# A transformer block in one kernel: where the up-projection's operands are read, split and kept

## The chip, the cores and the metric

The kernel runs on one core of one Trainium2 chip. The metric is device microseconds of one execution. Before the change three executions took 1883.05, 1883.9 and 1880.56 us, with a median of 1883.05 us. Times inside an execution are counted from the start of its span.

## The reference

The reference is one transformer block for 2048 tokens of width 1024, in fp32: linear attention with a learned feature map (32 heads of 32), then a dense layer with ReLU of width 3584. Both halves normalise first and add to their input.

```python
x = A_x
h = x + _A_ref(_layernorm(x), A_wqkv, A_w_phi, A_wo)
h2 = h + _B_ref(_layernorm(h), B_w1, B_w2)

# _A_ref: q, k, v = split(x @ wqkv); per head
phi_q = concat(softmax(q @ w_phi), softmax(-(q @ w_phi)))      # the same for k
o = phi_q @ (phi_k.T @ v) / (phi_q @ sum(phi_k) + 1e-6)        # then o @ wo
# _B_ref
relu(x @ w1) @ w2
```

## The kernel before

**Products in three parts.** Every fp32 operand is held as two fp32r parts: a high part, which ScalarE (ACT) writes as a rounded copy, and a low part, which VectorE (DVE) or GpSimd (POOL) writes as operand minus high part. A product is three matmuls (`mm3`): line 182 is high by high, 183 high by low, 184 low by high. Weights go through `Units`: SP loads a unit of 256 KB into one of six raw buffers, ACT writes its high part (line 125) and DVE or POOL its low part (line 129), into one of ten buffers. The load of a further unit waits until a raw buffer has been split.

**Stages.** Keys, values and queries come first, to about 520 us, then attention, then the output projection `wo` to 806 us. The up-projection runs from 806 to 1345 us and the down-projection to the end.

**The dense layer.** Both its products use a scheme of Strassen's kind: seven block products in place of eight. The normalised h is therefore kept as seven operands, the blocks 1, 5, 6, 2, 7, 3, 4 in the order of their first use (`UP`). Each block is 128 x 2 x 4 x 512 elements in SBUF (`hT[m]`: high and low part, four slices of 128 rows, 512 tokens). The tokens are worked in two halves. "First half" below is tokens 0 to 1023 (b = 0).

**How the first half's operands come about.** `ln_pair(i, stage)` takes two tiles of 128 tokens, for i = 0 to 3: it loads h, takes statistics, normalises, transposes on TensorE and forms the sums. `ln_store(i, j)` writes each of the seven results to DRAM (`hs[0, m]`, shape 128 x 4 x 4 x 128), for tile pair i. `h_load(0, m, g)` reads the two tile pairs 2g and 2g+1 of block m back into the low half of `hT[m]`; `h_high` (line 825, ACT) copies it to the high half, and `h_low` (line 829, DVE) subtracts that in place. TensorE reads all 512 tokens of both parts in every product, so both g have to be done before a block's second matmul.

The first half writes `hs[0, m][:, i]`: 2 KB of one partition in one piece. It reads with two transfers of 256 KB per `h_load`, and each of these writes pieces of 512 B into SBUF. The second half (`far_store`, line 805, and line 817) writes four pieces of 512 B per partition and reads with one transfer of 512 KB, in pieces of 1 KB.

**The order.** No scheduler reorders anything. `when(step, f, ...)` puts a call at a step, and a step is three matmuls. Each engine and the SP queue take their instructions in the order in which the calls are made, and wait in that order. After each step `W.advance` may issue a split and the next unit's load. `up0` is the up-projection's first step. The steps that the change touches are written as offsets from it:

```python
step = up0 + (8 * j + (-62, -32)[g] if j < 4 else 6 * (j - 4) + 10 + 2 * g)
high = up0 + (8 * j + (-48, -19)[g] if j < 4 else 6 * (j - 4) + 20 + 2 * g)
```

`j` counts the blocks in the order `UP`, so j = 4, 5, 6 are blocks 7, 3, 4. Each block is used for eight steps (two pairs of weight units p), so block j is needed first at step 8j. The low part is written 2 steps after the high one, or 5 for the last three blocks. The loads of weights that fall between, written as offsets of the same kind, stand at steps -31, -27, -23 and so on to -3, then 4, 8, 12, 16, 20, 24, 28. In the steps -39 to 1 the last items of `wo` also put in their additions (`wo_add`, line 691), their statistics (`far_stats`, lines 749 and 752), stores of h (line 698) and loads of x (line 658).

**Memory.** Pools are opened and closed in stages. A later pool lies on the bytes of earlier ones, and its tiles wait for the last use of the tiles beneath. The pool `hp` holds x and h of the output projection (`xh`, four buffers), one buffer of attention, the sums `s12` and `s4l`, and the statistics `hst` of the second half's tiles (eight of 48 B). Tiles take their place in the pool in the order in which they are first asked for, so `hst` lies last. On the same bytes the pool `mlp` later puts blocks 7, 3 and 4 and, behind them, `c11` and the other results of the up-projection. Before the change, block 4 lies on `xh`, the buffer of attention, `s12` and a part of `s4l`, and the first `c11` on the rest of `s4l` and on `hst`.

Of the kernel before, what the change touches and what calls it, by code (L numbers as in the profile page):

```python
# [9 lines left out]
F32 = mybir.dt.float32  # L10
# [5 lines left out]
P = 128  # L16
# [124 lines left out]
def kernel(  # L141
# [12 lines left out]
    v, act, pool, pe, sp = nc.vector, nc.scalar, nc.gpsimd, nc.tensor, nc.sync  # L154
# [18 lines left out]
    def f32(ap):  # L173
        return ap.bitcast(F32)
# [27 lines left out]
    hs = {(b, m): dram.tile([P, 4, 4, P], F32, name=f"hs{b}_{m}") for b in range(2) for m in UP}  # L202
# [535 lines left out]
    def ln_store(i, j):  # L738

        x1, x2 = (xnt["h", 4 * r + i] for r in range(2))  # L740
        s12, s4 = sums[0, i]
        m, t = ((1, x1[:, 0:512]), (5, s12[:, 0, :]), (6, s12[:, 1, :]), (2, x1[:, 512:]), (7, x2[:, 0:512]),
                (3, s4), (4, x2[:, 512:]))[j]
        sp.dma_start(hs[0, m][:, i], t.rearrange("p (k n) -> p k n", k=4))

    def far_stats(t, hf):
        if hf == 0:
# [6 lines left out]
    hst = {}  # L754
# [52 lines left out]
    sums, hT = {}, {}  # L807

    def h_load(b, m, g):

        cols = slice(2 * g * P, 2 * (g + 1) * P)
        if b == 0:
            lo = hT[m][:, 1, :, cols].rearrange("p k (i n) -> p k i n", i=2)
            for i in range(2):
                sp.dma_start(f32(lo[:, :, i, :]), hs[b, m][:, 2 * g + i])
            return
        sp.dma_start(f32(hT[m][:, 1, :, cols]), hs[b, m].rearrange("p k i n -> p k (i n)")[:, :, cols])

    def h_parts(m, g):
# [116 lines left out]
    def item(gen, *args, keys):  # L936
        items.append((gen, args + (keys,)))
        steps.extend((k,) for k in keys)
        return len(items) - 1
# [11 lines left out]
    for b, tiles in enumerate(groups):  # L951
        for hf in range(2):

            pairs = b == 0 and hf == 0
            for j in range(0, 4, 2 if pairs else 1):
# [3 lines left out]
                for half in range(2):  # L959
                    n = item(wo_pair, tiles[j:j + 2], hf, half, keys=[("wo", hf, 4 * half + k // 2) for k in range(8)])  # L960
# [26 lines left out]
    def when(step, f, *args):  # L987

        if step < 8 * first_up:
            do(step // 8, step % 8, f, *args)  # L990
        else:
            do(first_up + (step - 8 * first_up) // 4, step % 4, f, *args)
# [4 lines left out]
    for t in range(1, NT):  # L997
        n = t - 1 if t < HT else q_n[1, t - HT] + 1
# [62 lines left out]
    def to_wo():  # L1061
        nonlocal hp
        right.close()
        opool[1] = wos.enter_context(tc.tile_pool(name="oT1", bufs=1, side="right", reuse_waits="tile"))
        hp = wos.enter_context(tc.tile_pool(name="hp", bufs=2, side="right", reuse_waits="tile"))

    def to_far():
        far = wos.enter_context(tc.tile_pool(name="wofar", bufs=6, side="right", reuse_waits="tile"))
        W.far = Ring(far, 6, [P, 2, 512], F32R, "wf")
# [23 lines left out]
    do(q_n[0, 0], -1, to_half)  # L1093
    do(last_kv + 4, -1, to_attention)
    do(wo_first, -1, to_wo)
    do(wo_first + 2, -1, to_far)
    do(wo_n[12, 0], -1, to_ln2)
# [47 lines left out]
    up0 = 8 * first_up  # L1145
    when(up0 + 26, far_scale)
    for i in range(4):
        near, far = wo0 + 64 + 40 * i, up0 + 60 + 68 * i
        ln2 = NEAR.get(i, (0, 9, 12, 17, 24, 25, 26, 27, 29, 36))
        for stage in range(9):  # L1150
            when(near + ln2[stage], ln_pair, i, stage)
        for stage in range(7):
            when(far + FAR[stage], far_pair, i, stage)
        for j in range(7):
            when(near + ln2[9] + j // 2, ln_store, i, j)
            when(far + FAR[7] + j, far_store, i, j)
    assert wo_n[8, 0] + 10 < first_up

    def up_step(b, p, m):

        return up0 + 4 * (up_n[b, p, m] + 1 - first_up)

    for j, m in enumerate(UP):

        for g in range(2):
            step = up0 + (8 * j + (-62, -32)[g] if j < 4 else 6 * (j - 4) + 10 + 2 * g)
            high = up0 + (8 * j + (-48, -19)[g] if j < 4 else 6 * (j - 4) + 20 + 2 * g)
            when(step, h_load, 0, m, g)
            when(high, h_high, m, g)
            when(high + (2 if j < 4 else 5), h_low, m, g)  # L1170
            step = up_step(0, NP - 1, m) + 2 * j
            when(step + 3 * g, h_load, 1, m, g)
            when(step + 22 + 4 * g, h_high, m, g)
            when(step + 25 + 4 * g, h_low, m, g)
# [13 lines left out]
    for n, (w, p, j) in enumerate((w, p, j) for w in (1, 2) for p in range(NP) for j in range(2)):  # L1188
        step = sums_at[n]
# [7 lines left out]
    for b in range(2):  # L1197
        for m in DOWN:
            n = down_n[b, m, NP - 1] + 1
            name, more = {1: "x1", 5: "x4", 6: "x2", 4: "x3"}.get(m), \  # L1200
# [109 lines left out]
```

## Time and profile before

| | before |
|---|---|
| median of three executions | 1883.05 us |
| the profiled execution's own time | 1883.67 us |
| its span | 1881.9 us |
| TensorE busy | 1871.4 us (99%) |
| VectorE, GpSimd, ScalarE busy | 1070.6, 973.1, 739.0 us |
| DMA, mean over the span | 230 GB/s |

The profiled execution's own time is 1.8 us over its span. Rows in the prediction come from four kinds of views. A wait reads "engine line waited for: us in total, times, longest". A row of the order in time reads "start, length, engine, line, operation, out<-in, shapes, count", and in brackets how long the engine stood idle in front of it and what ended that. A row of a stretch reads "length, then for each engine busy us and instructions, then the granted TensorE clock (1.00 is full), the busy share of the DMA engines and GB/s". A group of one tile's instructions reads "line, engine, operation, out<-in, count: shortest/median/longest in ns, first and last start". "SPq" is the queue of the engine that issues the DMAs; its rows are the issue, not the transfer. A matmul's length overlaps with the next one's, so its cost is the distance between starts.

### The profile page before, as it was taken

How to read it: one execution, taken by the hardware profiler on the slowest of the kernel's cores; microseconds unless marked ns; L12 is line 12 of the kernel's file. 1: busy time of each engine (PE TensorE's matmuls, PEld its weight loads, DVE VectorE, ACT ScalarE, POOL GpSimd, SP SyncE). 2: the span in 40 equal slices, each digit the busy share in tenths (PEclk: the TensorE clock that was granted, in tenths of full speed). 3: DMA queues.
4: the chain of work that ended last, by engine and by line, in shares of the span. 5: the costliest groups of instructions: out<-in, count | busy, mean ns of one | idle time of the engine just before them, and what ended most of it. 6: DMA issues, size and time to landing. Idle time of an engine off the chain costs nothing.

```text
span 1881.9 us, 31799 instructions
## 1 busy us (share of the span) xinstructions
PE 1871.4 (99%) x11608; PEld 1535.3 (82%) x11608; DVE 1070.6 (57%) x1695; ACT 739.0 (39%) x1271; POOL 973.1 (52%) x959
## 2 busy tenths in 40 slices
PE   9999999999999999999999999999999999999999
PEld 7877788888787888878888888888888888888887
DVE  7788688677689777555554563444433333343333
ACT  5322245222233122255455554444444444444442
POOL 4887744888946988333233222222344444444443
PEclk9999999999999999999999999999999999999999
DMA  6888788656565666887888985666677677767775
GB/s 225 290 293 289 227 296 258 199 190 200 185 217 177 203 226 221 259 258 217 258 254 263 320 273 176 192 191 215 210 238 215 204 228 238 238 213 219 216 216 178
DMA packets 303277, 432.17 MB, mean 230 GB/s; under 512 B 24208, under 2 KB 165520, under 8 KB 303120
## 3 DMA queue, kind: packets, MB, share of 16 engines
q1 hardware_dynamic: 286224, 413.36, 70.0%
q10 hardware_dynamic: 16896, 16.78, 2.7%
q8 instruction: 91, 1.49, 0.3%
q14 instruction: 66, 0.54, 0.1%
HBM read 292.68 MB, written 137.36 MB: 229 GB/s over the span
## 4 chain that ended last, share of the span: by engine, by line
PE 95%; DMA 2%; POOL 1%; DVE 1%; issue 0%; ACT 0%; SPq 0%; DVEq 0%; ACTq 0%; POOLq 0%
PE mm L182 25%; PE mm L183 24%; PE mm L184 24%; PE ac L183 4%; PE ac L182 4%; PE ac L184 4%; PE tp L183 2%; PE tp L184 2%; PE tp L182 2%; PE tp L245 1%; PE ac L464 1%; PE tp L633 1%; DMA hT<-hs 1%; DMA hs<-xin 1%; PE ac L633 1%; POOL w L129 0%
## 5 line engine op out<-in xcount | busy, mean ns | idle before, releaser
L129 POOL TENSOR_TENSOR w<-raw,w 128x512 fp32r<-128x512 f32 x353 | 469.2, 1331 | 719.8 <-ACT w L125 674.8
L125 ACT ACTIVATE w<-raw 128x512 fp32r<-128x512 f32 x686 | 409.0, 626 | 508.0 <-PE mm L184 235.0
L129 DVE TENSOR_TENSOR w<-raw,w 128x512 fp32r<-128x512 f32 x333 | 271.4, 816 | 519.5 <-ACT w L125 514.1
L182 PE MATMUL mm<-w,xT 128*128 128x512 f32 x768 | 305.3, 398 | 0.0
L183 PE MATMUL mm<-w,xT 128*128 128x512 f32 x768 | 299.8, 390 | 0.6 <-POOL w L400 0.4
L184 PE MATMUL mm<-w,xT 128*128 128x512 f32 x768 | 299.3, 390 | 0.0
L183 PE MATMUL mm<-hT,w 128*128 128x512 f32 x672 | 262.1, 390 | 2.8 <-DVE hT L829 2.8
L182 PE MATMUL mm<-hT,w 128*128 128x512 f32 x672 | 262.2, 390 | 0.0
L184 PE MATMUL mm<-hT,w 128*128 128x512 f32 x672 | 262.0, 390 | 0.0
L362 POOL TENSOR_TENSOR b<-b 128x256 f32<-128x256 f32 x176 | 143.5, 816 | 55.1 <-DMA b<-in_w_dram 36.9
L182 PEld LDWEIGHTS mm<-w,xT 128*128 128x128 f32 x768 | 144.2, 188 | 33.9 <-issue 2.9
L184 PEld LDWEIGHTS mm<-w,xT 128*128 128x128 f32 x768 | 144.2, 188 | 30.7
L183 PEld LDWEIGHTS mm<-w,xT 128*128 128x128 f32 x768 | 144.3, 188 | 29.9 <-POOL w L129 1.0
L182 PE MATMUL mm<-w 128*128 128x512 f32 x392 | 152.5, 389 | 0.0
L183 PE MATMUL mm<-w 128*128 128x512 f32 x392 | 152.5, 389 | 0.0
L184 PE MATMUL mm<-w 128*128 128x512 f32 x392 | 152.5, 389 | 0.0
L183 PEld LDWEIGHTS mm<-hT,w 128*128 128x128 f32 x672 | 126.6, 188 | 29.6 <-DVE hT L829 3.3
L184 PEld LDWEIGHTS mm<-hT,w 128*128 128x128 f32 x672 | 126.6, 188 | 26.4
L182 PEld LDWEIGHTS mm<-hT,w 128*128 128x128 f32 x672 | 126.4, 188 | 26.3
L182 PEld LDWEIGHTS mm<-w 128*128 128x128 f32 x392 | 73.6, 188 | 15.3
L183 PEld LDWEIGHTS mm<-w 128*128 128x128 f32 x392 | 73.6, 188 | 15.3
L184 PEld LDWEIGHTS mm<-w 128*128 128x128 f32 x392 | 73.6, 188 | 15.2
(184 smaller groups left out, 3147.9 us busy)
## 6 DMA issues: line engine op xcount, KB each, us to landing
raw<-t SPq DMA_DIRECT2D x224, 256.0 KB, 3.9
raw<-ad SPq DMA_DIRECT2D x196, 256.0 KB, 3.0
raw<-in_w_dram SPq DMA_DIRECT2D x168, 256.0 KB, 3.1
ad<-c SPq DMA_DIRECT2D x112, 256.0 KB, 3.6
b<-in_w_dram SPq DMA_DIRECT2D x44, 512.0 KB, 6.0
t<-b SPq DMA_DIRECT2D x44, 512.0 KB, 4.8
ad<-s SPq DMA_DIRECT2D x84, 256.0 KB, 3.9
ed<-qe ACTq DMA_DIRECT2D x32, 512.0 KB, 4.4
```

Of the source, the lines that this page charges most:

```text
L125: nc.scalar.activation(w[:, 0, :], raw[1], AF.Copy)
L129: eng.tensor_tensor(out=w[:, 1, :], in0=raw[1], in1=w[:, 0, :].bitcast(F32), op=ALU.subtract)
L182: pe.matmul(ps, a_hi, b_hi, start=first, stop=False, skip_group_check=more)
L183: pe.matmul(ps, a_hi, b_lo, start=False, stop=False, skip_group_check=more)
L184: pe.matmul(ps, a_lo, b_hi, start=False, stop=last, skip_group_check=more)
L245: pe.transpose(pt[:, k, :], xn[:, (4 * j + k) * P:(4 * j + k + 1) * P], ident)
L362: pool.tensor_tensor(out=tsum[*u, *out], in0=tsum[*u, *a], in1=tsum[*u, *b], op=ALU.subtract)
L464: pe.matmul(kv_ps[s][g][32 * i:32 * (i + 1), 0:64], vt[:, 32 * h:32 * (h + 1)], phi[:, 64 * h:64 * (h + 1)], start=first, stop=last)
L633: pe.matmul(banks[g][32 * c:32 * (c + 1), j * P:(j + 1) * P], kvL[rows, 4 * q + 2 * sd + h // 4, 32 * (h % 4):32 * (h % 4 + 1)], phT_of[u ...
```

## The change

There are five edits. (1) The first half's stores write `hs[0, m][:, :, i]`, so the four slices of a tile pair lie apart. (2) The special form of `h_load` for b = 0 goes, and every read is one transfer of 512 KB. (3) The second reads (g = 1) of the first four blocks stand at -29 in place of -32, and their high parts at -15 in place of -19, so 14 steps behind the read. (4) The reads of the last three blocks stand 6 steps sooner and their high and low parts 2 steps sooner, so the high part is again 14 steps behind the read. (5) `to_wo` asks for one `hst` tile at once, so that the statistics take the first bytes of `hp`; block 4 then lies on the statistics, and the first `c11` exactly on `s4l`.

```diff
-        sp.dma_start(hs[0, m][:, i], t.rearrange("p (k n) -> p k n", k=4))
+        sp.dma_start(hs[0, m][:, :, i], t.rearrange("p (k n) -> p k n", k=4))
...
         cols = slice(2 * g * P, 2 * (g + 1) * P)
-        if b == 0:
-            lo = hT[m][:, 1, :, cols].rearrange("p k (i n) -> p k i n", i=2)
-            for i in range(2):
-                sp.dma_start(f32(lo[:, :, i, :]), hs[b, m][:, 2 * g + i])
-            return
         sp.dma_start(f32(hT[m][:, 1, :, cols]), hs[b, m].rearrange("p k i n -> p k (i n)")[:, :, cols])
...
         hp = wos.enter_context(tc.tile_pool(name="hp", bufs=2, side="right", reuse_waits="tile"))
+        hp.tile([P, 2, 6], F32, name="hst", bufs=8)
...
-            step = up0 + (8 * j + (-62, -32)[g] if j < 4 else 6 * (j - 4) + 10 + 2 * g)
-            high = up0 + (8 * j + (-48, -19)[g] if j < 4 else 6 * (j - 4) + 20 + 2 * g)
+            step = up0 + (8 * j + (-62, -29)[g] if j < 4 else 6 * (j - 4) + 4 + 2 * g)
+            high = up0 + (8 * j + (-48, -15)[g] if j < 4 else 6 * (j - 4) + 18 + 2 * g)
             when(step, h_load, 0, m, g)
             when(high, h_high, m, g)
             when(high + (2 if j < 4 else 5), h_low, m, g)
```

## The prediction

> **What bounds the kernel now.** I read the page's busy times first, then the waits of TensorE (engine, line, what it waited for: total us, times, longest), then stretches of the span (length, busy time and instructions of each engine, clock, DMA share, GB/s), then the order of single instructions in the stretch that stands out.
>
> ```profile
> PE 1871.4 (99%) x11608; PEld 1535.3 (82%) x11608; DVE 1070.6 (57%) x1695; ACT 739.0 (39%) x1271; POOL 973.1 (52%) x959
> PE mm L183 <- DVE hT L829: 2.8, 1, 2.8
> PE tp L1229 <- POOL ones L1225: 1.6, 1, 1.6
> PE tp L245 <- ACT xn L238: 1.3, 1, 1.3
> 799.00:846.00 47.00, 44.16 (x217) 35.89 (x216) 26.70 (x35) 25.33 (x38) 18.61 (x20) 0.96 0.87 262
> 846.00:893.00 47.00, 47.00 (x209) 38.93 (x208) 27.61 (x34) 23.67 (x43) 15.29 (x11) 1.00 0.76 214
> ```
>
> TensorE is busy 1871.4 of 1881.9 us; apart from the first microseconds its one long wait is for hT, the up-projection's operand, at the subtraction of line 829. The stretch that holds this wait is also the one with a clock under 1.00. So the change can gain there and nearly nowhere else; everything else it does can only add a wait of TensorE.
>
> ```profile
> 828.80 0.39 PE L182 MATMUL mm<-hT,w 128*128 128x512 f32 x1
> 832.03 0.50 PE L183 MATMUL mm<-hT,w 128*128 128x512 f32 x1 [2.84 <-DVE hT L829]
> 836.24 0.39 PE L182 MATMUL mm<-hT,w 128*128 128x512 f32 x1
> 836.48 0.39 PE L183 MATMUL mm<-hT,w 128*128 128x512 f32 x1
> 832.00:836.00 4.00, 3.97 (x10) 3.15 (x11) 4.00 (x5) 3.36 (x5) 1.13 (x1) 0.57 1.07 305
> ```
>
> **What the stall costs.** Matmuls start 0.23 us apart (836.24 to 836.48), so the one at 832.03 was due at 829.03: 3.00 us. Behind it the granted clock is 0.57 for 4.00 us, which loses 4.00 x 0.43 = 1.72 us. Together 4.7 us, if the subtraction is ready by 829.03 and no clock is lost.
>
> It is block 7 (step 32 after the up-projection's start at 806.21; a step is three matmuls, 0.68 us). Why it is late, on SP, ACT and DVE:
>
> ```profile
> 813.11 5.22 SPq L337 DMA_DIRECT2D raw<-t  x2
> 818.43 0.93 SPq L815 DMA_DIRECT2D hT<-hs  x2
> SPq L337 <- DVE w L129: 4.4, 1, 4.4
> 813.75 0.60 ACT L852 ACTIVATE c<-mm 128x512 f32<-128x512 f32 x1 [2.78 <-DVE mv L752]
> 824.93 1.06 ACT L825 ACTIVATE hT<-hT 128x1024 fp32r<-128x1024 f32 x1 [4.24 <-DMA hT<-hs]
> 827.40 1.06 ACT L825 ACTIVATE hT<-hT 128x1024 fp32r<-128x1024 f32 x1 [0.93 <-DMA hT<-hs]
> 828.37 0.61 ACT L125 ACTIVATE w<-raw 128x512 fp32r<-128x512 f32 x1
> 829.01 0.69 DVE L129 TENSOR_TENSOR w<-raw,w 128x512 fp32r<-128x512 f32 x1 [9.33 <-ACT w L125]
> 829.62 2.35 DVE L829 TENSOR_TENSOR hT<-hT 128x1024 fp32r<-128x1024 f32 x2
> ```
>
> SP issues one weight load at 813.11, then stands 4.4 us, because the next one needs a raw buffer that a DVE split frees; the reads of block 7 stand behind that load. They land about 6 us after issue, ACT copies the high parts at 824.93 and 827.40, and DVE subtracts until 831.97, behind a split that waits for ACT. In front of this, ACT's first take of c11 waited 2.78 us for line 752: the far tiles' statistics, whose bytes c11 reuses.
>
> **The change, part by part.** (1) Last three blocks. Loads go 6 steps sooner: block 7 from steps 10 and 12 to 4 and 6, block 3 to 10 and 12, block 4 to 16 and 18. In SP's written order the weight load of step 8, the one that waits 4.4 us, now comes behind block 7. So block 7 follows the issue at 813.11: about 813.5 and 814.0, not 818.43 and 819.96.
>
> ```profile
> L815 SPq DMA_DIRECT2D hT<-hs x28: 370/498/1534, 764.3 to 830.6; - x28
> L817 SPq DMA_DIRECT2D hT<-hs x14: 524/530/810, 1048.8 to 1091.5; - x14
> L825 ACT ACTIVATE hT<-hT x28: 1043/1051/1063, 773.6 to 1104.8; 128x1024 fp32r<-128x1024 f32 x28
> L829 DVE TENSOR_TENSOR hT<-hT x28: 1201/1218/2320, 775.0 to 1107.7; 128x1024 fp32r<-128x1024 f32 x28
> DMA to landing us min/median/max: 5.5/7.0/8.6
> ```
>
> The last line is of the 14 whole-size reads of the second half (line 817), the form that the first half now takes: 7.0 us median, 8.6 worst. From 814.0 that is 821.0 to 822.6. Then ACT: high, a split, high, a split (1.05 + 0.61 + 1.05 + 0.61 = 3.3, partly before the second landing, so some 2.3 behind it), and DVE 0.69 + 1.22: done at 825.2 to 826.8. Due is 829.03, so 2.2 to 3.8 us are left; with the longest subtraction of the row (2.32) still 1.1. The last two blocks follow by 8 steps (5.4 us) each and have the same lead. What is passed: the weight loads of steps 8 to 24 come behind up to three reads (0.53 us of issue each); their splits stand at steps 32 and later and their use at 60 and later, so 2 us there cost nothing. If that cover were gone, it would be those 2 us.
>
> (2) One read in place of two: 14 x (2 x 0.498 - 0.530) = 6.5 us of SP's time less, spread over 764 to 831. The stores must now scatter:
>
> ```profile
> L744 SPq DMA_DIRECT2D hs<-xin x16: 320/426/1196, 680.8 to 791.8; - x16
> L805 SPq DMA_DIRECT2D hs<-xin x16: 519/630/1027, 892.5 to 1032.9; - x16
> 790.00:800.00 10.00, 10.00 (x46) 8.29 (x45) 3.32 (x5) 2.39 (x4) 3.18 (x3) 1.00 1.02 343
> 824.00:830.00 6.00, 5.19 (x52) 3.77 (x50) 0.99 (x2) 3.88 (x7) 0.00 (x0) 1.00 1.11 302
> ```
>
> The second half's stores already have the new form (line 805): 0.2 us more of SP each, 28 x 0.2 = 5.7 us, in four bursts of seven. In the queue, mostly 2 KB pieces move at 343/1.02 = 336 GB/s, mostly 512 B pieces at 302/1.11 = 272. Seven stores of 0.26 MB take 5.5 us at the one and 6.7 at the other: up to 1.2 us per burst, less what reads in 1 KB pieces give back. None of the first three bursts has a reader soon; the fourth (785 to 792) counts in (3).
>
> (3) First four blocks, second halves: loads 3 steps later, high and low 4 later. On SP the read of block 1 passes a weight load and a load of x; on ACT its high part lets one split go first; on DVE its subtraction passes an addition with its statistics. Block 1 is needed at 806.43.
>
> ```profile
> 806.43 0.39 PE L183 MATMUL mm<-hT,w 128*128 128x512 f32 x1
> 796.20 0.69 DVE L691 TENSOR_TENSOR xh<-mm,xh 128x512 f32<-128x512 f32 x1 [8.41 <-DMA hd<-xh]
> 800.81 1.22 DVE L829 TENSOR_TENSOR hT<-hT 128x1024 fp32r<-128x1024 f32 x1 [1.15 <-ACT hT L825]
> 802.44 0.69 DVE L691 TENSOR_TENSOR xh<-mm,xh 128x512 f32<-128x512 f32 x1 [0.40 <-DMA hd<-xh]
> 803.16 0.70 DVE L749 BATCH_NORM_STATS2 hst<-xh 128x6 f32<-128x512 f32 x1
> 803.96 0.21 DVE L752 BATCH_NORM_AGGREGATE mv<-hst 128x2 f32<-128x12 f32 x1
> 804.09 0.64 DVE L129 TENSOR_TENSOR w<-raw,w 128x512 fp32r<-128x512 f32 x1
> ```
>
> Now the subtraction runs at 800.81, ahead of the addition at 802.44. Behind it, it starts when the split starts now, 804.09, and ends at 805.3: 1.1 us before 806.43. The high part fits: a read about 2 us later than now lands near 802 and is copied by 803. The addition starts when an earlier store of h lands; up to 1.2 us from (2) leaves 0 to 1.1 us. I cost it at nothing, with the bounds 0 and, if the store lands 2 us late, a gap of 0.9 plus 1.72 of clock, 2.6 us. Blocks 5, 6 and 2 follow by 8 steps each, with the same additions in front, and have more room. A gain is excluded: TensorE waits for nothing there now.
>
> (4) Statistics' place. No instruction more. c11 no longer lies on the statistics but on a sum stored about 791, so ACT's 2.78 us go. Block 4's tile now lies on the statistics, last read at 813.7; its load comes about 818. I take nothing beyond (1): the ACT wait is no wait of TensorE, and my 813.5 does not use it. The moved buffers of x and h serve a stage in which TensorE never waits.
>
> **Sum.** The profiled execution took 1883.67 us (span 1881.9): 1883.67 - 4.7 = 1879.0. The median of the three runs, 1883.05, is 0.6 lower: 1878.4.
>
> [...] The 2.84 us gap is followed by the clock of 0.57. [...] Here the row decides: every other 47 us stretch up to the kernel's end has 1.00, and gaps of 0.3 and 0.5 us (next fence) left it at 1.00.
>
> ```profile
> 470.00:517.00 47.00, 46.71 (x321) 37.13 (x320) 32.06 (x62) 12.56 (x23) 42.87 (x45) 1.00 0.58 183
> 564.00:611.00 47.00, 46.54 (x610) 37.49 (x623) 45.67 (x76) 15.10 (x27) 31.07 (x34) 1.00 0.54 182
> ```
>
> **Rivals.**
> A (my forecast): the stall goes, nothing takes its place. 1878.4. Chance 0.58.
> B: a smaller wait comes in its place, at 806 for block 1 or 812 for block 5, for the reason in (3). For: 0 to 1.1 us of room, DMA share about 1. Against: fewer issues, and ACT is freed earlier. 0.3 to 2.6 us: 1878.7 to 1881.0, with two such gaps 1882. Chance 0.21.
> C: the clock falls all the same. 1883.05 - 3.0 = 1880.05. Against: the fall stands directly behind the gap. Chance 0.04.
> D: the change does not do what it says; block 7 still lands late, because the queue is full, not SP held (DMA share near 1 around it). Then the 5 us of earlier issue shrink to under 2: a stall of 1 us or more with its clock, 1880.5 to 1883. Against: a wait of SP for a buffer, not for a landing, stands in front of the reads. Chance 0.06.
> E: slower. One mechanism: the addition ahead of block 1's subtraction waits for its store as the one at 796.20 did, 8.41 us in place of 0.40. The subtraction then ends at 813.3, a gap of 6.9 plus 1.72, less 4.7: +3.9, 1887.0. It decides from a gap of 3.0 on (no gain left). For: the moved read and the scattered stores sit in the same queue. Against: now it waits 0.40. Chance 0.11.
>
> **Numbers.** 0.2%, about what a measurement tells from no change, is 3.8 us. A is 0.25%; the three runs spread over 3.3 us, so I let one in six of A read as no change: faster 0.58 x 0.83 = 0.48, plus a third of B (0.07): 0.55. Same: 0.10 of A, 0.13 of B, C, D: 0.33. Slower: E and a trace of B, 0.12. Range: A's own is 1875.9 (1880.56 - 4.7) to 1880.5; with B, C and D it reaches 1884, and E stays out.
>
> **What would show it.** The wait of line 183 for line 829 at 829 gone, clock 1.00 in all stretches; block 7's reads issued right behind one weight load about 813 to 814; no ACT wait of a c11 take for line 752; block 1's last subtraction at 804 to 806.4. I am wrong if TensorE waits for line 829 near 806 or 812, or if a clock below 1.00 stays.

## The result, and the profile after

| | before | after |
|---|---|---|
| median | 1882.36 us (20 executions, 1880.56 to 1885.7) | 1879.31 us (20 executions, 1879.11 to 1879.53) |
| the profiled execution's own time | 1883.67 us | 1879.26 us |
| its span | 1881.9 us | 1877.5 us |

The ratio is 0.9983, with a 95% interval of 0.9976 to 0.999: the change makes the kernel 3.05 us faster (0.16%). Forecast were 1878.4 us and a gain of 0.25%. The time lies in the predicted range, 0.9 us above the forecast. By the bound of 0.2% that the prediction set, the gain counts as no change (which it gave a chance of 0.33, and faster 0.55), although the interval leaves 1 out.

Two differences have to be kept apart. The two profiled executions differ by 4.4 us, near the 4.7 us of the prediction's sum. The medians differ by 3.05. The experiments tell why.

The page and the waits of TensorE in the kernel after (engine, line, what it waited for: total us, times, longest), all that the trace has:

```profile
PE 1869.3 (100%) x11608; PEld 1533.9 (82%) x11608; DVE 1070.9 (57%) x1695; ACT 739.3 (39%) x1271; POOL 973.0 (52%) x959
PE tp L245 <- ACT xn L238: 1.6, 1, 1.6
PE tp L1225 <- POOL ones L1221: 1.6, 1, 1.6
PE tp L633 <- POOL ez L575: 0.5, 1, 0.5
PE mm L183 <- POOL w L400: 0.4, 1, 0.4
PE mm L183 <- POOL w L129: 0.3, 1, 0.3
```

The wait of 2.8 us for hT is gone, and no wait for hT has come in its place. Up to these places the code has five lines fewer, so lines 815 and 817 of before are 812 now, 825 is 820, 829 is 824, and 852 is 847.

The stretch that had clock 0.96 before, and the order in time on TensorE, SP, ACT and DVE (start, length, engine, line, operation, tiles, shapes, count, idle time in front):

```profile
799.00:846.00 47.00, 47.00 (x238) 38.72 (x237) 29.78 (x36) 27.22 (x41) 19.29 (x18) 1.00 0.88 288
```

```profile
806.56 0.39 PE L183 MATMUL mm<-hT,w 128*128 128x512 f32 x1
...
829.15 0.39 PE L183 MATMUL mm<-hT,w 128*128 128x512 f32 x1
```

```profile
812.07 0.32 SPq L337 DMA_DIRECT2D raw<-t  x1
812.48 1.20 SPq L812 DMA_DIRECT2D hT<-hs  x2
813.77 0.62 SPq L337 DMA_DIRECT2D raw<-t  x1
SPq L337 <- POOL w L129: 3.4, 1, 3.4
```

```profile
810.58 0.58 ACT L847 ACTIVATE c<-mm 128x512 f32<-128x512 f32 x1
...
818.58 1.06 ACT L820 ACTIVATE hT<-hT 128x1024 fp32r<-128x1024 f32 x1
```

```profile
803.88 1.20 DVE L824 TENSOR_TENSOR hT<-hT 128x1024 fp32r<-128x1024 f32 x1
...
824.13 1.22 DVE L824 TENSOR_TENSOR hT<-hT 128x1024 fp32r<-128x1024 f32 x1
```

TensorE's busy time fills the 47 us and the clock is 1.00. On SP both reads of block 7 are out by 813.7. The weight load behind them goes out at 813.77 without the 4.4 us in which the one before stood. SP is not free of such waits: the next weight load then stands 3.4 us for a split of POOL (the last row, a wait between 814 and 819), but block 7's reads are past it. ACT's first take of c11, at 810.58, has no wait in brackets; the high part of block 7's first half starts at 818.58, 6.3 us sooner than before. On DVE the subtraction of block 1 runs at 803.88. DVE finishes block 7 at 824.13 + 1.22 = 825.35, and TensorE uses it at 829.15: it has 3.8 us of room where it was 3.0 late.

### The profile page after: what moved, and what is told of

The parts are those of the page before. It is cut to its first block, busy times and chain, and to the rows that moved or that the text cites. A ratio compares the mean times of both kernels' runs of the same rounds, so it can differ in the third digit from the quotient of the medians.

```text
span 1877.5 us, 31764 instructions
## 1 busy us (share of the span) xinstructions
PE 1869.3 (100%) x11608; PEld 1533.9 (82%) x11608; DVE 1070.9 (57%) x1695; ACT 739.3 (39%) x1271; POOL 973.0 (52%) x959
## 4 chain that ended last, share of the span: by engine, by line
PE 98%; POOL 1%; DVE 0%; DMA 0%; ACT 0%; issue 0%; SPq 0%; POOLq 0%; ACTq 0%
PE mm L182 25%; PE mm L183 25%; PE mm L184 25%; PE ac L182 4%; PE ac L184 4%; PE ac L183 4%; PE tp L182 2%; PE tp L184 2%; PE tp L183 2%; PE tp L245 1%; PE ac L464 1%; PE tp L633 1%; PE ac L633 1%; POOL w L129 0%; PE tp L290 0%; PE mm L290 0%
```

## The experiments

The theory under test (the order theory): block 7's operand is late because its reads stand in SP's order behind a weight load that waits for a buffer. Rivals are that ACT's wait for the statistics passes the delay on, that the form or the number of the transfers makes it, and that the gain has another source than this stall. Unless said otherwise, each experiment is the kernel before with one edit.

### The last three blocks' steps alone

```diff
-            step = up0 + (8 * j + (-62, -32)[g] if j < 4 else 6 * (j - 4) + 10 + 2 * g)
-            high = up0 + (8 * j + (-48, -19)[g] if j < 4 else 6 * (j - 4) + 20 + 2 * g)
+            step = up0 + (8 * j + (-62, -32)[g] if j < 4 else 6 * (j - 4) + 4 + 2 * g)
+            high = up0 + (8 * j + (-48, -19)[g] if j < 4 else 6 * (j - 4) + 18 + 2 * g)
```

> Only the steps of the last three blocks are changed; stores, reads, the first four blocks and the statistics stay as before. My theory (block 7 is late because its reads are written behind the weight load that waits for a raw buffer): block 7's reads follow the weight load issued about 813, the wait of line 183 at 829 is gone, clock 1.00, and the time is that of the full change, 1879.3 us, 3 us under before. Rival A (the head of the delay is ACT's 2.78 us wait of the first c11 take for the statistics, and everything behind it is late in any order): ACT's wait is still there at about 811 to 814, block 2's high part comes behind it, and a wait of 0.5 to 2 us stays at 829: 1880.5 to 1882. Rival T (the pairs of 256 KB reads are what is slow): two reads of block 7 still land 2 us or more apart and the wait shrinks only by a half.

Measured: 1879.22 us (10 executions, 1878.92 to 1879.83) against 1881.7, ratio 0.9984 (0.9974 to 0.9993). It is as fast as the whole change. SP, ACT and DVE in order of time:

```profile
812.92 0.38 SPq L337 DMA_DIRECT2D raw<-t  x1
813.39 2.47 SPq L815 DMA_DIRECT2D hT<-hs  x4
817.77 0.33 SPq L337 DMA_DIRECT2D raw<-t  x1
```

```profile
813.55 0.60 ACT L852 ACTIVATE c<-mm 128x512 f32<-128x512 f32 x1 [2.67 <-DVE mv L752]
```

```profile
824.93 1.22 DVE L829 TENSOR_TENSOR hT<-hT 128x1024 fp32r<-128x1024 f32 x1
```

The four reads (two halves of block 7, two transfers each) are out ahead of the weight load, which still has to stand until 817.77. The low part ends at 826.15, 3.8 us ahead of its use at 829.91 in this trace. ACT's wait for the statistics is still there, 2.67 us, and the reads still have the old form. So neither of these has to go for the stall to end: the order alone is enough. The edit also moves the high and low parts, by two steps or 1.4 us; that is less than the 3.8 us of room, so the reads decide.

### All edits but that one

```diff
-        sp.dma_start(hs[0, m][:, i], t.rearrange("p (k n) -> p k n", k=4))
+        sp.dma_start(hs[0, m][:, :, i], t.rearrange("p (k n) -> p k n", k=4))
...
-        if b == 0:
-            lo = hT[m][:, 1, :, cols].rearrange("p k (i n) -> p k i n", i=2)
-            for i in range(2):
-                sp.dma_start(f32(lo[:, :, i, :]), hs[b, m][:, 2 * g + i])
-            return
...
+        hp.tile([P, 2, 6], F32, name="hst", bufs=8)
...
-            step = up0 + (8 * j + (-62, -32)[g] if j < 4 else 6 * (j - 4) + 10 + 2 * g)
-            high = up0 + (8 * j + (-48, -19)[g] if j < 4 else 6 * (j - 4) + 20 + 2 * g)
+            step = up0 + (8 * j + (-62, -29)[g] if j < 4 else 6 * (j - 4) + 10 + 2 * g)
+            high = up0 + (8 * j + (-48, -15)[g] if j < 4 else 6 * (j - 4) + 20 + 2 * g)
```

> Everything of the change but the steps of the last three blocks, which stay at 10 and 20. My theory: the reads stand behind the weight load of step 8 again; if that load waits about as long as before, the stall stays at 2 to 3 us and the time is that of before, 1882.4. Rival A (edit 5 frees ACT, which frees the raw buffer): the weight load goes out about 814 and block 7 is read about 814.5 and 815.5, so its low part is done before 829 with or without the earlier steps: 1879.3, as the full change. In the trace of the changed kernel that weight load goes out at 813.77, which speaks for A.

Measured: 1879.67 us (1879.14 to 1880.56), ratio 0.9988 (0.9979 to 0.9998), and no wait of TensorE for hT in the profile. The expectation that the stall stays fell. SP and DVE:

```profile
811.97 2.00 SPq L337 DMA_DIRECT2D raw<-t  x2
814.06 0.53 SPq L812 DMA_DIRECT2D hT<-hs  x1
...
818.18 0.32 SPq L337 DMA_DIRECT2D raw<-t  x1
818.55 0.53 SPq L812 DMA_DIRECT2D hT<-hs  x1
```

```profile
826.49 2.35 DVE L824 TENSOR_TENSOR hT<-hT 128x1024 fp32r<-128x1024 f32 x2
```

Here the weight load still stands ahead of block 7's reads, but it waits under 2 us, so the first half's read goes out at 814.06, 4.4 us sooner than before. The low part needs both halves, though, and the second half's read still stands behind a wait of SP (3.5 us, for a split of POOL): it goes out at 818.55, 1.4 us sooner than before, as one transfer that lands 5.7 us after issue. Before, the second of its two transfers went out at 820.4 and landed 6.9 us after issue. The low part ends at 828.84, 0.3 us ahead of its use. So the stall also ends without the earlier steps, by several smaller gains together. Rival A has the time right, but its second read was to go out at 815.5, and the statistics alone, further down, give nothing. Three single parts were then tried.

### Single reads with the stores that they need

```diff
-        sp.dma_start(hs[0, m][:, i], t.rearrange("p (k n) -> p k n", k=4))
+        sp.dma_start(hs[0, m][:, :, i], t.rearrange("p (k n) -> p k n", k=4))
...
-        if b == 0:
-            lo = hT[m][:, 1, :, cols].rearrange("p k (i n) -> p k i n", i=2)
-            for i in range(2):
-                sp.dma_start(f32(lo[:, :, i, :]), hs[b, m][:, 2 * g + i])
-            return
```

> Only the stores' form and the single 512 KB reads are changed; steps and statistics stay as before. Rival T (the transfers): block 7's second half lands about 1 us sooner behind its issue, and SP has 0.45 us less per read to issue; with fewer transfers in flight block 2 is also read sooner. The stall falls to 1 us or less: 1880 to 1880.7. My theory: the weight load of step 8 still holds SP to 817 or so, block 7 lands about 824 to 825.5, the low part ends about 830: a stall of 1 to 2 us, with or without the clock, 1880.5 to 1882.4. Slower than before by more than 1 us would mean that the scattered stores cost by themselves.

Measured: 1880.59 us (1880.13 to 1881.08), ratio 0.9992 (0.9983 to 1.0001). The stall is shorter, and no execution lost clock. SP and TensorE:

```profile
812.11 4.55 SPq L337 DMA_DIRECT2D raw<-t  x2
816.76 0.53 SPq L812 DMA_DIRECT2D hT<-hs  x1
```

```profile
830.02 0.50 PE L183 MATMUL mm<-hT,w 128*128 128x512 f32 x1 [0.76 <-DVE hT L824]
```

SP is still held for 4 us, but comes to it a microsecond sooner, and the read follows at 816.76 in place of 818.43. The gap is 0.76 us in place of 2.84, so by the size of the gap rival T came, although SP is held as the order theory had it. The form of stores and reads is thus a cause of a part of the stall, and the order is not the only one.

### The first four blocks' second halves alone

```diff
-            step = up0 + (8 * j + (-62, -32)[g] if j < 4 else 6 * (j - 4) + 10 + 2 * g)
-            high = up0 + (8 * j + (-48, -19)[g] if j < 4 else 6 * (j - 4) + 20 + 2 * g)
+            step = up0 + (8 * j + (-62, -29)[g] if j < 4 else 6 * (j - 4) + 10 + 2 * g)
+            high = up0 + (8 * j + (-48, -15)[g] if j < 4 else 6 * (j - 4) + 20 + 2 * g)
```

> Only the second reads of the first four blocks and their high and low parts are moved, in the old form of two reads. My prediction took this as worth nothing. Theory now: it frees ACT for one split before block 1's high part, so SP is not held 3 us at 800 and comes 1 us sooner to the reads behind; the stall at 829 shrinks by at most 1 us: 1880.5 to 1882. If it costs, a wait of line 183 near 806 shows up. The rival that this edit is the larger half of what the change gains without the last three blocks would show as 1879.5 to 1880.

Measured: 1880.19 us (1879.37 to 1882.08), ratio 0.9989 (0.9979 to 0.9999), no execution with lost clock. SP in order of time, and the wait of TensorE (total us, times, longest):

```profile
814.80 0.87 SPq L337 DMA_DIRECT2D raw<-t  x2
815.77 0.93 SPq L815 DMA_DIRECT2D hT<-hs  x2
```

```profile
PE mm L183 <- DVE hT L829: 0.6, 1, 0.6
```

The two weight loads go out one behind the other, and block 7's first read follows at 815.77, 2.7 us sooner than before. SP still stands in front of them, but 2.9 us in place of 4.4, and for a split of POOL. Why it no longer stands there for DVE is seen on DVE. The split whose buffer SP waits for, and the subtraction of block 2 next to it, in the kernel before:

```profile
816.16 1.23 DVE L829 TENSOR_TENSOR hT<-hT 128x1024 fp32r<-128x1024 f32 x1 [2.44 <-ACT hT L825]
817.30 0.69 DVE L129 TENSOR_TENSOR w<-raw,w 128x512 fp32r<-128x512 f32 x1
```

And in this experiment (the first row is the split, the second block 2's subtraction):

```profile
813.93 1.40 DVE L129 TENSOR_TENSOR w<-raw,w 128x512 fp32r<-128x512 f32 x1 [0.30 <-ACT w L125]
816.66 1.23 DVE L829 TENSOR_TENSOR hT<-hT 128x1024 fp32r<-128x1024 f32 x1 [1.33 <-ACT hT L825]
```

Before, the split stood behind a subtraction that waited 2.44 us for its high part. Four steps later, high part and subtraction come behind the split, which runs 3.4 us sooner and frees SP's buffer. The half that ends last gains less from this: its second transfer goes out at 819.9 in place of 820.4, behind another wait of SP for POOL (2.2 us), but lands 5.7 us after issue in place of 6.9; why it lands faster is not shown. So an edit to the first four blocks, whose operands are never late, is worth 1.8 us in the medians through block 7, between the 1 us that was expected at most and the rival's 1879.5 to 1880 us.

### The statistics' place alone

```diff
+        hp.tile([P, 2, 6], F32, name="hst", bufs=8)
```

> Only the statistics' place is changed (one line). Rival A: the c11 take runs about 811 instead of 813.75, the split behind it and so the weight load of step 8 come up to 2.8 us sooner, block 7's low part ends about 829.2 instead of 832.0: the stall shrinks to 0 to 0.5 us without loss of clock, 1879.3 to 1880. My theory in its strict form (order alone): block 2's high part still waits for its read at 815, so the split behind it and the load move by less than 1 us; a stall of 2 us or more stays, 1881 to 1882.4.

Measured: 1882.22 us (1880.43 to 1883.9), ratio 1.0002 (0.9992 to 1.0011). ACT, SP and TensorE:

```profile
810.97 0.58 ACT L852 ACTIVATE c<-mm 128x512 f32<-128x512 f32 x1
814.65 1.06 ACT L825 ACTIVATE hT<-hT 128x1024 fp32r<-128x1024 f32 x1 [3.10 <-DMA hT<-hs]
```

```profile
812.99 4.93 SPq L337 DMA_DIRECT2D raw<-t  x2
818.01 0.94 SPq L815 DMA_DIRECT2D hT<-hs  x2
```

```profile
831.14 0.50 PE L183 MATMUL mm<-hT,w 128*128 128x512 f32 x1 [1.96 <-DVE hT L829]
```

ACT's take of c11 no longer waits, but ACT then waits 3.10 us for a read that it had to wait for anyway. SP's order is as before, and the stall is there. The wait of 2.78 us stood in front of another wait; taking it away moved the read of block 7 by 0.4 us and the time by nothing that can be told from no change.

### The last three blocks' steps later

```diff
-            step = up0 + (8 * j + (-62, -32)[g] if j < 4 else 6 * (j - 4) + 10 + 2 * g)
-            high = up0 + (8 * j + (-48, -19)[g] if j < 4 else 6 * (j - 4) + 20 + 2 * g)
+            step = up0 + (8 * j + (-62, -32)[g] if j < 4 else 6 * (j - 4) + 14 + 2 * g)
+            high = up0 + (8 * j + (-48, -19)[g] if j < 4 else 6 * (j - 4) + 24 + 2 * g)
```

> The kernel before with reads, high and low parts of the last three blocks 4 steps (2.7 us) later. My theory of the clock (a longer gap makes the loss of clock more frequent): the gap grows to 3.5 to 5.5 us, nearly every run has the lowered clock (3.4 us at half, 1.7 us lost), and the time is 1.5 to 5 us over before: 1883.5 to 1887. Rival (the clock is lost by chance, whatever the gap): a third of the runs has it, as before. If the reads' place in the order does not matter, since SP is held by the weight load and not by the steps, the gap stays at 2 to 3 us and the time within 1 us of before.

Measured: 1882.64 us (1880.41 to 1885.39), ratio 0.9998 (0.9989 to 1.0007). SP, and the waits of TensorE for hT:

```profile
812.71 5.99 SPq L337 DMA_DIRECT2D raw<-t  x3
818.79 0.94 SPq L815 DMA_DIRECT2D hT<-hs  x2
```

```profile
PE mm L183 <- DVE hT L829: 1.7, 2, 0.9
PE mm L183 <- DMA hT<-hs: 0.8, 1, 0.8
```

One longer gap, as expected, did not come, nor a third of the executions with lost clock, as the rival had it: one of ten lost some, and TensorE has three shorter waits, 2.5 us in all. The median is that of before only because two things cancel: fewer executions lose clock, and the nine that lose none have a median of 1882.5 us, 1.2 over those of the kernel before that lose none (1881.29). Four steps later in the written order are only one more weight load on SP, and this one went out at once: the read goes out at 818.79 in place of 818.43. What sets the time of block 7's read is how long SP is held, not the number of the step.

### Block 7 alone, behind two more weight loads

```diff
-            step = up0 + (8 * j + (-62, -32)[g] if j < 4 else 6 * (j - 4) + 10 + 2 * g)
-            high = up0 + (8 * j + (-48, -19)[g] if j < 4 else 6 * (j - 4) + 20 + 2 * g)
+            step = up0 + (8 * j + (-62, -32)[g] if j < 4 else 6 * (j - 4) + (18 if j == 4 else 10) + 2 * g)
+            high = up0 + (8 * j + (-48, -19)[g] if j < 4 else 6 * (j - 4) + (24 if j == 4 else 20) + 2 * g)
```

> The kernel before with block 7 alone moved: its reads from steps 10 and 12 to 18 and 20, high and low parts 4 steps later; blocks 3 and 4 stay. My theory (gap and lost clock add up, and the longer the gap, the more often the clock is lost): block 7 is read behind two more weight loads and a read of block 3, lands 2 to 3 us later, and the gap at 829 grows to 4.5 to 6 us in one piece; all or nearly all runs lose the clock; the time is 1879.3 + 4.5 to 6 + 1.7 = 1885.5 to 1887. Rival (the clock falls by chance in a third of the runs, whatever the gap): 1884 to 1885.5 in two thirds of the runs. Rival (the place in the order does not matter): as before, 1882.

Measured: 1887.44 us (8 executions, 1886.68 to 1888.64) against 1883.13, ratio 1.0025 (1.0014 to 1.0036). SP, TensorE, and the stretch behind the gap (length, busy time and instructions of each engine, clock, DMA share, GB/s):

```profile
813.18 6.92 SPq L337 DMA_DIRECT2D raw<-t  x4
820.19 4.95 SPq L815 DMA_DIRECT2D hT<-hs  x6
...
826.02 2.91 SPq L815 DMA_DIRECT2D hT<-hs  x4
```

```profile
834.16 0.79 PE L182 MATMUL mm<-hT,w 128*128 128x512 f32 x1 [4.91 <-ACT hT L825]
```

```profile
832.00:840.00 8.00, 5.38 (x12) 3.90 (x13) 4.77 (x5) 6.54 (x9) 1.99 (x1) 0.60 0.61 157
```

This is the same stall made longer. Four weight loads stand in front, and by the order of the steps the first two of the six transfers at 820.19 are a read of block 3. Block 7's first half follows them, and its second half goes out only at 826.02, where it went out at 819.96 before. The gap is 4.91 us, and all eight executions lost clock. The time follows the read's place on SP in this direction too, but the edit puts another read in front as well as weight loads. It came out 0.4 us over the expected 1885.5 to 1887.

### The first four blocks' second halves still later, on the kernel after

```diff
-            step = up0 + (8 * j + (-62, -29)[g] if j < 4 else 6 * (j - 4) + 4 + 2 * g)
-            high = up0 + (8 * j + (-48, -15)[g] if j < 4 else 6 * (j - 4) + 18 + 2 * g)
+            step = up0 + (8 * j + (-62, -21)[g] if j < 4 else 6 * (j - 4) + 4 + 2 * g)
+            high = up0 + (8 * j + (-48, -7)[g] if j < 4 else 6 * (j - 4) + 18 + 2 * g)
```

> The changed kernel with the second reads of the first four blocks at -21 in place of -29, and their high parts at -7, so 8 steps later still. In the changed kernel block 1's subtraction ends at 805.1 and is needed at 806.56, so it has 1.5 us. Moved behind one more weight load, one load of x and one more addition, which starts about 806.3 with its statistics, it ends about 809 to 810: a wait of line 183 of 2 to 3.5 us near 806.6. My theory (the price of such a wait is the gap, plus 1.7 us where the clock falls): 1881.5 to 1884.5. Rival (room elsewhere absorbs it): no wait at 806 and 1879.3.

Measured: 1881.1 us (1880.65 to 1881.79), 0.9995 (0.9985 to 1.0004) of the kernel before and 1.8 us over the kernel after. TensorE in order of time:

```profile
806.87 0.39 PE L182 MATMUL mm<-hT,w 128*128 128x512 f32 x1
808.55 0.50 PE L183 MATMUL mm<-hT,w 128*128 128x512 f32 x1 [1.30 <-DVE hT L824]
```

This is the place of rival B. The matmul at 808.55 was due at 806.87 + 0.23 = 807.10: 1.45 us late, in a kernel 1.8 us slower. The wait behind block 1's subtraction is real once the steps go far enough, but it is shorter than the expected 2 to 3.5 us, and its price is about the gap alone: none of the ten executions lost clock.

### The kernel before, three times more

The kernel is unchanged, so there is no diff. First in ten executions:

> The kernel before itself, profiled again. Two of its groups of runs differ in the granted clock: in the runs of the last comparison 11 of 31 had a mean clock of 0.999 and 1882.7 to 1884.7 us, 20 had 1.000 and 1880.7 to 1882.7 us. My theory: the gap at 829 is there in every run, 2 to 3 us, and the halved clock behind it only in some; the first profile was one with it. So the median costs 2 to 3 us of gap and not 4.7. Expected: ratio 1.000, and a gap of 1.5 to 3 us in the profile, with a clock of 1.00 behind it if the run is below 1882.5 us, with 0.5 to 0.6 if above 1883. Rival: the gap itself is only there in the slow group: then a profile at 1881 us shows no wait of line 183.

Measured: 1883.13 us (1880.95 to 1886.6), ratio 1.0007 (0.9998 to 1.0016). The profiled execution is the slowest of them, with an own time of 1886.6. Its matmul behind the stall, the first one back at full spacing, and the stretch around them:

```profile
833.66 0.79 PE L183 MATMUL mm<-hT,w 128*128 128x512 f32 x1 [3.01 <-DVE hT L829]
...
839.79 0.39 PE L182 MATMUL mm<-hT,w 128*128 128x512 f32 x1
```

```profile
832.00:840.00 8.00, 6.34 (x15) 4.98 (x16) 7.41 (x9) 5.98 (x9) 1.55 (x1) 0.57 1.06 318
```

From 833.66 to 839.79 TensorE starts 14 matmuls in 6.13 us. At the full pace of three in 0.68 us it would take 3.18, so this execution lost 2.95 us to the clock, not the 1.72 us of the prediction.

Then in one execution each:

> The kernel before itself, one more profile. My theory: a wait of line 183 for line 829 of 1.5 to 3 us stands near 829 in every execution; the clock behind it is 1.00 in an execution of 1880.5 to 1882.7 us (three in five) and near 0.57 over some 4 us in one of 1882.8 us and more. Rival (without the lowered clock there is no gap either): a profile at 1881 us has no wait of line 183 for line 829.

> The same kernel before, a further profile, with the same expectation: gap always, 1.5 to 3 us; lowered clock behind it in some executions only, and then 1.7 us on top.

The first took 1883.74 us. Its matmul behind the gap, and the first one that is spaced at about half speed (0.43 us from start to start in place of 0.23):

```profile
832.02 0.50 PE L183 MATMUL mm<-hT,w 128*128 128x512 f32 x1 [2.71 <-DVE hT L829]
...
833.52 0.63 PE L183 MATMUL mm<-hT,w 128*128 128x512 f32 x1
```

The second took 1881.22 us. The same matmul, and the stretch:

```profile
831.16 0.50 PE L183 MATMUL mm<-hT,w 128*128 128x512 f32 x1 [1.58 <-DVE hT L829]
```

```profile
832.00:836.00 4.00, 4.00 (x19) 3.33 (x18) 4.00 (x5) 2.60 (x4) 0.25 (x1) 1.00 1.09 327
```

So the same program has executions with a gap near 3 us and the clock at half behind it, and executions with a shorter gap and full clock. The gap itself comes out differently: of the 1.26 us between 1.58 and the 2.84 of the prediction's profile, 0.4 are an earlier issue of block 7's last transfer (820.1 against 820.4), 0.5 its faster landing (6.4 us after issue against 6.9) and 0.4 a later TensorE (due at 829.42 against 829.03). The mean granted clock that each run lists divides the executions (0.999 or less: some clock lost; 1.000: none, or less than 0.9 us, since the figure has three digits). Of the 73 executions of the kernel before that served as comparisons in the three sets of runs, 42 lost none, with medians of 1881.20, 1881.29 and 1881.34 us in the three sets, and 31 lost some, with medians of 1883.73, 1883.65 and 1883.52. The ten more of this section divide into 4 and 6. The kernel after stands at 1879.31, so it is 1.9 to 2.0 us under the one group and 4.2 to 4.4 under the other, and its own 20 executions spread over 0.4 us.

That gap and clock go together within the kernel before is seen in four profiles. Across kernels the share of executions with lost clock goes with the gap of the profiled execution:

| kernel | gap in its profile, us | executions that lost clock |
|---|---|---|
| after; last three blocks sooner alone | none | 0 of 30 |
| all edits but that one | none | 1 of 10 |
| first four blocks alone | 0.6 | 0 of 10 |
| single reads alone | 0.76 | 0 of 10 |
| after, first four blocks still later | 1.30 | 0 of 10 |
| last three blocks later | three gaps, 2.5 in all | 1 of 10 |
| statistics' place alone | 1.96 | 3 of 10 |
| before | 1.58, 2.71, 2.84, 3.01 | 31 of 73 |
| block 7 behind two more loads | 4.91 | 8 of 8 |

One row does not fit at first sight: of the kernel with all edits but the last three blocks' steps, one execution lost clock (1879.7 us, no longer than its median), though its profile has no gap. Its low part ends 0.3 us before it is due, so other executions may have a gap; no trace of that one exists.

## Why the prediction was right, and where it was not

**The stall and its cause: right.** The one long wait of TensorE was what the change could gain at, and it is gone. That the reads' place behind a held weight load is a sufficient cause is shown from both sides: block 7's reads moved ahead of it, with the stores, the form of the reads, the first four blocks and the statistics as before, give 1879.22 us, and moved behind two more loads and a read of block 3, 1887.44.

**Part (1), the last three blocks: right, with its numbers.** Predicted were reads at about 813.5 and 814.0; the two went out from 812.48 on, by 813.7. Predicted for the end of the low part was 825.2 to 826.8; it is 825.35, with 3.8 us left, the better end of the predicted 2.2 to 3.8. That is in part luck, since two misses cancel: the second read left 0.9 us sooner and landed at 820.1 (7.0 us after issue) where 821.0 to 822.6 was predicted, but the copies, splits and subtraction behind it took 5.2 us in place of 4.2. No clock is lost.

**The sum: the step that was mis-sized.** "Together 4.7 us" is right for the profiled execution, and 1883.67 - 1879.26 = 4.41 us is what the two profiles differ by. But the sum was then set against the median of three runs with a correction of only 0.6, as if each execution had a gap of 3.00 us and lost 1.72 us of clock. The clock is lost in 31 of 73 executions, and one profile without the loss has a gap of 1.58 in place of 2.84. Weighted by these executions the stall is worth (42 x 2.0 + 31 x 4.3) / 73 = 3.0 us, near the 3.05 between the medians, and not 4.7. The sum's first line, 1883.67 - 4.7 = 1879.0, was 0.3 us from the time of the kernel after; the 0.6 taken off behind it, for a median among executions with a smaller stall, made that 0.9. The three times known beforehand (1880.56 to 1883.9) already had a spread of 3.3 us; it was read as noise of the measurement, but it was for the most part the term itself, there in some executions and absent in others. The kernel after shows it: without the stall the spread is 0.4 us.

**Part (2), single reads: costed as a relief of SP's queue and possible DMA time; the relief also shortens the stall.** Alone it brings the first read of block 7 forward by 1.7 us and the gap to 0.76, a gain that the prediction did not cost. The feared lengthening of the bursts put no wait for hT on TensorE.

**Part (3), the first four blocks: the place right, the verdict wrong.** Block 1's subtraction was predicted at 804.09 to 805.3 and ran from 803.88 to 805.08, with 1.5 us of room where 1.1 was expected. But "A gain is excluded: TensorE waits for nothing there now" fell. Alone the edit is worth 1.8 us, at block 7. The prediction had the mechanism in its hand, "on ACT its high part lets one split go first", but followed it for block 1 alone. For block 2 the split that goes first is the one whose buffer SP waits for in front of block 7's reads. The mistake was to ask only who waits at the moved work, and not who waits for the work that now passes it.

**Part (4), the statistics: right.** ACT's wait is gone and nothing came of it (1.0002).

**Overdetermined.** The prediction gave the whole gain to part (1). Part (1) alone does bring all of it, but without it the other parts bring 1879.67. So "everything else it does can only add a wait of TensorE" fell. The prediction also kept SP's wait of 4.4 us for DVE's split and only put block 7 ahead of it. In the kernel after that wait is gone, and one of 3.4 us for POOL's split stands in its place, behind block 7's reads. With the first four blocks' steps alone SP waits 2.9 us for POOL.

**The rivals.** B did not come, but its mechanism exists: with the steps moved 8 further its gap appears at 807, and there it is 1.45 us without the 1.72 of clock that the prediction had added for a gap of 0.9. C and D fell with the clock of 1.00 and the reads at 812.48. E did not come.

**The row on the clock.** The row was right for the execution in which it stood, and the prediction was right to charge the lost clock to the gap: in the kernel after, without the gap, the clock is 1.00. In three profiles of the kernel before, gaps of 2.71 to 3.01 us were followed by the lower clock (matmuls 0.43 us from start to start, where the full pace is 0.23); in the fourth, a gap of 1.58 us was followed by a clock of 1.00. Why only a part of the executions of one program shows the loss stays open. The longest gap in these blocks without the loss was 1.96 us and the shortest with it 2.71, and the gap itself differs from one execution to the next.

## What to carry to other kernels

When an operand is late, look first at what stands in front of its load on the issuing queue: here a load that waited 4.4 us for a buffer held everything written behind it, and moving the late load in front of it (or making it wait less) was worth the gap, while a wait on another engine that only stood in front of a second wait was worth nothing. A gain that one profiled execution shows, above all one with lost clock in it, should be weighted by how many executions have it; a spread in the times of the kernel before can be a sign that the term comes and goes. An edit of the written order is costed for the work that now goes first, up to the place of the stall, not only where the moved work is used.

## What the runs showed of the hardware

The granted clock fell behind longer gaps and not behind shorter ones (0.57 over 4 us behind 2.84 us of gap, 1.00 behind 1.58). In the three kernels with one gap of at most 1.30 us in the profile no execution of 30 lost it, around 2 to 3 us a part did, and at 4.91 us all eight. In the single profiles every gap up to 1.96 us in the up-projection kept the clock and every one from 2.71 us on lost it; no profile has a gap between the two. The fall did not always come in the gap: in the execution with the gap of 2.71 us TensorE resumed at 832.02 at full speed (0.23 us from start to start), went to about half at 833.52 (0.43 us), 1.5 us after work had resumed, and was back at 836.9, 3.4 us later. At half speed that is, as an estimate, 1.7 us lost, the same as the prediction's 1.72 from another execution. The loss isn't always that size: the execution with the gap of 3.01 us lost 2.95 us. So a gap near 3 us cost 4.7 us in one execution and about 6 in another, and one of 1.30 cost about 1.5.
